# Engine per small SBUF step named in the list, and the list planned anew with a VectorE/GpSimd lock

## Chip, cores and metric

One core of one Trainium2 chip runs the kernel. The metric is the time of one execution on the device in microseconds (us), as the median of several runs. Engines are named as in the profile: PE is TensorE (PEld its weight loads), DVE is VectorE, ACT is ScalarE, POOL is GpSimd, SP is SyncE, which issues nearly all DMAs.

## The reference

Two blocks are chained. The first is a linear attention with decay, over 4 batches, 8 heads, 768 tokens and head size 48; its output is read as a 3072 x 384 matrix, which the second block feeds through a multiplicative feed-forward net (width 1024).

```python
for t in range(S):                                     # S = 768, all in float32
    cur = einsum('bhd,bhe->bhde', u * k[t], v[t])
    y[t] = einsum('bhd,bhde->bhe', r[t], state + cur)
    state = w * state + einsum('bhd,bhe->bhde', k[t], v[t])
x = y.transpose(0, 2, 1, 3).reshape(B * S, H * D)      # 3072 x 384
out = (((x @ w1) * (x @ w2)) @ w3) @ w_out             # 384 -> 1024 -> 1024 -> 384
```

## The kernel before

**Attention.** The 24 units are 6 chunks of 128 tokens by 4 batches, and unit n is visited once. Its k, r and v are loaded by SP (`kr.n`, `v.n`). Step `k.n` (`scale`, L459) multiplies k and r by powers of the decay, one 128x768 product of two SBUF operands. The results are turned so that the head dimension lies on the partitions: on PE for the first five units (`T`, `R`, with `t`, `r` on ACT), later by 32x32 blocks on DVE (`x`), a round trip through DRAM on SP (`y`, `z`) and a copy on ACT (`l`). PE then forms the sums for the state (`U`) and the pair products (`A`); DVE updates the state (`i`, `j`, each with a product of two SBUF operands at L633 in all but the first chunk's first half) and masks the pairs (`m`); PE multiplies by the state (`S`) and by the pairs (`V`), with a small fence on DVE in between (`fe`, L720). For units from 5 on the term of u is made apart: `d.n` and `e.n` (L468 and L471, 128x384 products, k r u), `f.n` (sums per head on DVE) and `g.n` (eight ACT scalings of v, or for unit 5 one DVE product, `h.5`). `vs.n` (L715) copies the odd heads' v to the other half of the partitions. `Y`, `yt` and `yx` add up, turn and store the unit's output as columns of x.

**Weights.** The inputs of the feed-forward net arrive as pairs of 32-bit words. Each of the 32 pieces (8 of 768 columns for w1 and w2, 8 of 384 for w_out, 16 of 512 for w3) is fetched by SP into one of three buffers (`W.i`, L272), and converted in five steps: `M` and `L` on ACT, `N` (L419), `H` (L422) and `Q` (L429, an addition of integers of two SBUF operands) on DVE. The w3 pieces are turned on DVE (`G`) and multiplied with w_out on PE (`F`, L445).

**Feed-forward net.** Chunk 0 uses plain products (`a`, `b`). Chunks 1 to 5 use a scheme with twenty products for eight blocks (`pa`, `pb`, L949), which needs 22 sums of weight blocks for each of w1 and w2 (`wa`, `wb`) and 11 sums of token blocks for each chunk (`xs`), all 128x256 sums of two SBUF operands (L921). `ga` and `gb` take the products out of PSUM, on ACT and DVE. The last product uses seven for eight (`P`, L834), with sums of 128x512 blocks of two SBUF operands (`s`, L816 and L819), and `E` takes it out. `D` stores.

**What sets the order.** Everything after the set-up follows one list written out by hand of a planner, `ORDER`: 1580 words such as `k.4` or `S.5/20` (after the slash, PSUM banks). Each engine issues its own instructions strictly in the order of the list, and waits by semaphores only. The engine of a step is fixed in the code of the step: `scale`, `total` (Q) and the masks run on DVE; `rk`, `rku` (d, e), `odd_values` (vs), `sum_of_ab` (s) and `sums_of_x` (xs) on POOL; `sums_of_w` alternates, even sums on DVE, odd ones on POOL; `place` (g) runs on ACT. `ps` (L934) sets up three PSUM banks just ahead of the first `pa`; it ends the early part of the list.

Of the kernel before, what the change touches and what calls it, by code (L numbers as in the profile page):

```python
# [29 lines left out]
N.3 L.4 a.0.1.0/1 H.3 Y.2/23 W.7 Y.3/05 k.4 yt.2/2 L.3 yt.3/3 b.0.0.0/0 yx.2/2 Q.3 W.6 c.0.1.0/1 yx.3/3 R.4/5 j.2/4  # L30
M.5 a.0.2.2/2 N.5 H.5 Q.4 L.5 a.0.1.1/1 Q.5 W.8 M.7 N.7 b.0.2.2/3 c.0.2.2/2 kr.7 H.7 u.0.0.0/0 L.7 N.6 M.6 T.4/4 Q.7
W.10 a.0.4.2/2 c.0.1.1/1 H.6 M.8 ub N.8 L.6 H.8 k.5 L.8 W.9 b.0.1.0/0 t.4/4 Q.6 a.0.5.2/1 W.11 x.5 M.10 e.5 N.10 H.10
v.5 L.10 y.5 r.4/5 b.0.5.2/4 Q.10 W.13 M.9 Q.8 c.0.5.2/1 N.9 ku.4 H.9 u.0.2.2/3 L.9 U.4/51 vs.5 M.11 A.4 W.12 k.6
c.0.4.2/2 Au.4 a.0.0.1/3 N.11 H.11 cz.1 L.11 Q.9 b.0.3.2/2 M.13 W.14 u.0.1.0/0 f.5 N.13 d.6 M.12 Q.11 kr.8 N.12 H.13
e.6 a.0.3.2/0 z.5 u.0.5.2/4 L.13 i.4/5 H.12 W.16 x.6 L.12 a.0.6.2/4 c.0.3.2/0 f.6 M.14 m.4 d.7 W.15 Q.13 wb.1 N.14
H.14 b.0.6.2/5 vs.4 j.4/1 L.14 l.5 Q.14 W.17 mo.4 M.16 Q.12 S.4/01 y.6 N.16 c.0.6.2/4 v.6 U.5 H.16 A.5 fe.4/1 M.15
N.15 V.4/01 L.16 H.15 b.0.4.2/4 u.0.3.2/2 L.15 W.19 Q.15 u.0.6.2/5 M.17 W.18 i.5 Y.4/01 c.0.0.1/3 a.0.7.2/2 N.17 m.5
j.5 z.6 k.7 yt.4/5 H.17 b.0.7.2/0 yx.4/5 u.0.4.2/4 L.17 Q.16 W.20 Q.17 G.0 b.0.1.1/1 M.18 v.7 N.18 c.0.7.2/2 F.0/3
N.19 H.18 x.7 L.18 M.19 W.21 h.5 H.19 Q.18 L.19 M.20 N.20 W.22 Q.19 vs.7 H.20 vs.6 b.0.0.1/5 G.1 y.7 L.20 e.7 l.6 W.23
u.0.7.2/0 F.1/4 M.21 N.21 u.0.0.1/5 H.21 Q.20 L.21 M.22 N.22 W.24 wa.0 H.22 Q.21 L.22 X.0/3 G.2 W.25 U.6 f.7 S.5/20  # L40
M.23 A.6 cz.0 d.8 N.23 F.2/5 H.23 k.8 L.23 g.6 W.26 i.6 Q.22 Q.23 z.7 M.24 G.3 M.25 N.25 kr.9 F.3/3 H.25 N.24 L.25
H.24 X.2/5 W.28 Q.25 M.26 X.1/4 fe.5/0 N.26 L.24 H.26 m.6 L.26 j.6 l.7 W.29 Q.24 S.6/54 X.3/3 x.8 U.7 W.27 A.7 fe.6/4
G.4 V.5/20 V.6/54 M.28 y.8 Q.26 F.4/3 kr.10 m.7 Y.5/20 N.28 M.29 u.0.1.1/1 H.28 N.29 L.28 H.29 W.31 Q.28 L.29 Q.29
wb.3 yt.5/2 X.4/3 P.0.1.0/0 e.8 G.6 yx.5/2 M.27 N.27 F.6/1 H.27 k.9 L.27 W.30 i.7 Q.27 G.5 v.8 z.8 wa.2 x.9 F.5/3
# [1075 lines left out]
```

## Time and profile before

| | |
|---|---|
| median of 3 runs (us) | 487.74 (484.59 to 488.23) |
| the profiled execution: its own time | 482.68 |
| its span, first to last instruction | 480.9 |
| busy: PE, DVE, ACT, POOL (us) | 454.3, 313.4, 200.6, 187.0 |
| mean granted clock of PE | 0.994 |

Busy time is that of an engine's own instructions. PE's matmuls are pipelined, so a busy PE need not run at its peak. The chain of waits is the list of work that ended last, followed back from the end. A window's "DMA share" is the busy share of the sixteen DMA engines. The rows the prediction uses stand in a section of their own below.

### The profile page before, as it was taken

What the parts mean: (1) busy time and instruction counts of PE and PEld (TensorE: products, weight loads), DVE (VectorE), ACT (ScalarE), POOL (GpSimd) and SP (SyncE); (2) the same over time, 40 slices, a digit from 0 to 9 for tenths busy, and PEclk for the clock granted to TensorE, in tenths of its full rate; (3) what the DMA queues carried; (4) which work ended last, traced back from release to release, by engine and by line L of the source; (5) the groups of instructions that cost most, each with busy time, mean ns of one, the idle gap of its engine ahead of it and who ended that gap; (6) DMA issues with size and microseconds to landing.
All of it is one profiled execution on the core that took longest, in us unless ns stands there. A gap on an engine that the chain in (4) does not pass through costs nothing.

```text
span 480.9 us, 12217 instructions
## 1 busy us (share of the span) xinstructions
PE 454.3 (94%) x4977; PEld 377.6 (79%) x4977; DVE 313.4 (65%) x596; ACT 200.6 (42%) x451; POOL 187.0 (39%) x228
## 2 busy tenths in 40 slices
...
GB/s 183 272 225 260 205 192 231 230 185 211 208 86 149 155 12 132 66 134 65 90 47 180 72 108 73 99 116 1 91 25 35 33 19 50 1 16 1 49 20 56
DMA packets 100482, 52.74 MB, mean 110 GB/s; under 512 B 79296, under 2 KB 89792, under 8 KB 100416
## 3 DMA queue, kind: packets, MB, share of 16 engines
...
q14 instruction: 25, 0.20, 0.1%
q10 hardware_dynamic: 624, 0.00, 0.1%
...
## 4 chain that ended last, share of the span: by engine, by line
PE 60%; DVE 18%; DMA 10%; issue 4%; ACT 3%; SPq 3%; POOL 0%; DVEq 0%; ACTq 0%
PE ps_fixed L949 22%; DMA raw<-in_moe_w_dram 7%; PE ps_b L949 6%; PE ps_a L949 5%; PE ps_s3t L834 3%; PE ps_s4b L834 3%; PE ps_a12b L834 3%; PE ps_a22t L834 3%; PE ps_s1t L834 2%; PE ps_a11b L834 2%; PE ps_s2t L834 2%; ACT t L426 2%; SPq L272 2%; DVE krs L459 2%; PE ps_y L708 2%
## 5 line engine op out<-in xcount | busy, mean ns | idle before, releaser
L816 POOL TENSOR_TENSOR raw<-abt,abt 128x512 f32<-128x512 f32 x12 | 16.5, 1379 | 144.6 <-DVE abt L982 129.9
L949 PE MATMUL ps_fixed<-xT,w 128*128 128x256 f32 x200 | 50.8, 381 | 0.0
L445 PE MATMUL ps_w<-wo,w3T 128*128 128x384 f32 x128 | 43.0, 490 | 2.1 <-DVE w3T L440 1.8
L949 PEld LDWEIGHTS ps_fixed<-xT,w 128*128 128x128 f32 x200 | 37.2, 190 | 4.8 <-ACT ps_fixed L966 0.5
L489 ACT ACTIVATE ynat<-vnat,dg 128x48 f32<-128x48 f32 x144 | 34.6, 330 | 14.9 <-PE ps_x L747 12.5
L445 PEld LDWEIGHTS ps_w<-wo,w3T 128*128 128x128 f32 x128 | 23.8, 190 | 18.6 <-ACT w3n L414 1.7
L715 POOL COPY vodd<-vnat 64x192 f32<-64x192 f32 x48 | 19.8, 412 | 45.4 <-DMA vnat<-in_v_dram 39.6
L468 POOL TENSOR_TENSOR ruk<-krin 128x384 f32<-128x384 f32 x19 | 21.5, 1129 | 37.7 <-DVE dg L475 26.7
L982 DVE TENSOR_TENSOR abt<-ps_fixed,abt 128x512 f32<-128x512 f32 x35 | 24.1, 688 | 16.2 <-PE ps_fixed L949 16.0
L426 ACT ACTIVATE t<-raw 128x512 uint32<-128x512 uint32 (+2 forms) x32 | 22.8, 714 | 24.1 <-DVE w3n L422 11.2
L980 ACT COPY abt<-ps_fixed 128x512 f32<-128x512 f32 x30 | 17.4, 589 | 29.9 <-PE ps_fixed L949 29.9
L459 DVE TENSOR_TENSOR krs<-krin,pn_in 128x768 f32<-128x768 f32 x24 | 26.4, 1104 | 1.6 <-ACT pn_in L342 1.1
L471 POOL TENSOR_TENSOR ruk<-ruk,ub 128x384 f32<-128x384 f32 x19 | 19.6, 1031 | 17.6 <-DMA ub<-in_u_dram 16.5
L545 ACT COPY kT<-tt 128x1024 f32<-128x1024 f32 x19 | 19.9, 1045 | 9.0 <-PE ps_y L708 4.2
L777 PE MATMUL ps_a<-xT,w 128*128 128x512 f32 (+1 forms) x60 | 22.6, 516 | 0.2
L777 PE MATMUL ps_b<-xT,w 128*128 128x512 f32 (+1 forms) x60 | 22.2, 509 | 0.0
L753 ACT COPY xT<-ps_x 128x384 f32<-128x384 f32 x24 | 11.4, 479 | 24.6 <-PE ps_x L747 14.6
L949 PE MATMUL ps_b<-x,w 128*128 128x256 f32 x80 | 20.8, 383 | 0.3 <-DVE ps_fixed L976 0.2
L949 PE MATMUL ps_fixed<-x,w 128*128 128x256 f32 x80 | 20.6, 380 | 0.0
L949 PE MATMUL ps_a<-x,w 128*128 128x256 f32 x80 | 20.6, 380 | 0.0
L834 PE MATMUL ps_a12b<-w,abt 128*128 128x192 f32 x96 | 18.7, 342 | 1.2 <-DVE u L862 1.2
L819 POOL TENSOR_TENSOR raw<-abt,raw 128x512 f32<-128x512 f32 x12 | 16.2, 1352 | 8.2 <-DVE abt L982 7.5
...
## 6 DMA issues: line engine op xcount, KB each, us to landing
...
```

The costliest lines, as they stand in the source:

```text
L426: nc.scalar.activation(out=part["t", i], in_=words(i)[0], func=COPY, scale=2.0 ** -29)
L445: nc.tensor.matmul(ps, lhsT=w3T[j][:, kc].rearrange("x b k -> x (b k)"), rhs=wo[kc], start=(kc == 0), stop=(kc == KF - 1))
L459: nc.vector.tensor_mul(krs[n % NS][:, which, :, :D], kr[:, which], pn[:, which, :, :D])
L468: (nc.gpsimd if fast else nc.vector).tensor_mul(ruk[n], krin[n % NIN][:, 0], krin[n % NIN][:, 1])
L471: (nc.gpsimd if fast else nc.vector).tensor_mul(ruk[n], ruk[n], ub)
L489: nc.scalar.activation(out=ynat[n][:, h, :], in_=vnat[n % NV][:, h, :], func=COPY, scale=dg[n][:, h:h + 1])
L545: nc.scalar.copy(out=turned(n).rearrange("x g p (z t) -> x (g p) z t", t=Q), in_=tts.rearrange("x z e t -> x e z t"))
L715: nc.gpsimd.tensor_copy(out=vodd[n % NV][rows(a)], in_=vnat[n % NV].rearrange("t (p i) d -> t i p d", i=2)[rows(1 - a), 1])
L777: nc.tensor.matmul(ps, lhsT=(w1 if x == "a" else w2)[:, z, q, js], rhs=xT[c][:, q, ts], start=(q == 0), stop=(q == KM - 1))
L834: nc.tensor.matmul(ps, lhsT=operand(c, j // 2, a)[:, j % 2, m * C:(m + 1) * C], rhs=w34[:, KH * (x == 1) + j, :DH] if x < 2 else made[b][: ...
L949: nc.tensor.matmul(bank_of(w, c, n)[:, i * TH:(i + 1) * TH], lhsT=of_weights(w, of_w)[:, i * P:(i + 1) * P], rhs=of_tokens(c, of_x), start ...
L982: nc.vector.tensor_mul(at(*more), flat(ps), at(*more))
```

## The change

Each word of the list can now carry an engine: `k.1@g` on GpSimd, `k.2@V` on VectorE, `vs.0@A` on ScalarE. The steps that read it are `k`, `Q`, `d`, `e`, `g`, `vs`, `s`, `wa`, `wb` and `xs`. The list has been planned anew by a planner that knows of a lock between VectorE and GpSimd; the whole order changes with it. The set of steps is the same but for `h.5`, which is now `g.5@V`, and two new steps: `Z.4` and `Z.3`, seven idle matmuls of `ident` by itself at the start (`busy_array`, in the code before, not used in the list). The numbers of steps by engine, before and after:

| step | DVE | POOL | ACT |
|---|---|---|---|
| k (24) | 24 to 12 | 0 to 12 | |
| Q (32) | 32 to 19 | 0 to 13 | |
| d, e (19 each) | 0 to 9, 0 to 10 | 19 to 10, 19 to 9 | |
| s (48) | 0 to 19 | 48 to 29 | |
| xs (55) | 0 to 18 | 55 to 37 | |
| wa, wb (44) | 22 to 25 | 22 to 19 | |
| g (19) | 1 to 7 | | 18 to 12 |
| vs (24) | | 24 to 14 | 0 to 10 |

```diff
 ORDER = """
-v.1 kr.2 W.1 uw k.1 k.0 T.1/0 T.0/1 N.0 M.0 R.0/2 W.2 U.0/34 r.0/2 H.0 vs.1 kr.3 t.0/1 R.1/5 i.0/3 vs.0 ku.0 U.1/21
-j.0/4 A.0 S.0/34 k.2 L.0 Au.0 i.1/2 r.1/5 W.3 m.0 t.1/0 S.1/25 mo.0 v.2 ku.1 R.2/0 N.1 A.1 j.1/1 M.1 Q.0 H.1 M.2 Au.1
...
+kr.2 k.1@g W.1 v.1 vs.0@A k.0 Z.4/1 T.0/0 R.0/1 t.0/0 R.1/2 N.0 M.0 T.1/3 uw U.0/45 v.2 r.0/1 H.0 A.0 W.2 L.0 k.2@V
+kr.3 ku.0 i.0/4 Z.3/1 T.2/0 Q.0@V S.0/14 j.0/5 Au.0 M.1 N.1 t.1/3 H.1 vs.1@A U.1/53 W.3 L.1 i.1/5 ku.1 W.4 Q.1@g j.1/3
...
+Q.20@g G.1 c.0.1.1/0 kr.8 N.22 F.1/2 wb.0@g u.0.5.2/1 M.21 H.22 vs.5@g wa.0@V L.22 N.21 l.6 x.7 W.25 Q.22@g M.23 f.7
+H.21 y.7 N.23 L.21 H.23 b.0.1.1/4 X.0/5 Q.21@g u.0.4.2/3 L.23 b.0.0.1/0 W.26 Q.23@g G.2 M.25 S.5/15 W.24 X.1/2 d.8@V
...
+        chosen_banks, chosen_side = [], [""]
+        sides = dict(V=nc.vector, A=nc.scalar, g=nc.gpsimd)
+        side = lambda other: sides.get(chosen_side[0], other)
...
         def total(i):
-            nc.vector.tensor_add(part[i], part[i], part["t", i])
+            side(nc.vector).tensor_add(part[i], part[i], part["t", i])
...
-                nc.vector.tensor_mul(krs[n % NS][:, which, :, :D], kr[:, which], pn[:, which, :, :D])
+                side(nc.vector).tensor_mul(krs[n % NS][:, which, :, :D], kr[:, which], pn[:, which, :, :D])
...
-            (nc.gpsimd if fast else nc.vector).tensor_mul(ruk[n], krin[n % NIN][:, 0], krin[n % NIN][:, 1])
+            side(nc.vector).tensor_mul(ruk[n], krin[n % NIN][:, 0], krin[n % NIN][:, 1])
...
-            if engine is nc.vector:
+            if side(nc.scalar) is nc.vector:
                 nc.vector.tensor_mul(ynat[n], vnat[n % NV], dg[n][:, :, None].to_broadcast([C, H, D]))
...
-                nc.gpsimd.tensor_copy(out=vodd[n % NV][rows(a)], in_=vnat[n % NV].rearrange("t (p i) d -> t i p d", i=2)[rows(1 - a), 1])
+                (nc.scalar.copy if side(nc.scalar) is nc.scalar else nc.gpsimd.tensor_copy)(out=vodd[n % NV][rows(a)], in_=vnat[n % NV].rearrange("t (p i) d -> t i p d", i=2)[rows(1 - a), 1])
...
-            engine = nc.gpsimd if fast else nc.vector
+            engine = side(nc.vector)
...
-            add_up((nc.vector, nc.gpsimd)[x % 2], WSUMS, x, lambda n: of_weights(w, n))
+            add_up(WSUMS, x, lambda n: of_weights(w, n))
...
-            add_up(nc.gpsimd, XSUMS, x, lambda n: of_tokens(c, n))
+            add_up(XSUMS, x, lambda n: of_tokens(c, n))
...
                     word, _, at = word.partition("/")
+                    word, _, chosen_side[0] = word.partition("@")
```

## Rows read from the trace of the kernel before

**Rows 1.** Windows: length, busy us (instructions) of PE, PEld, DVE, ACT, POOL; clock; DMA share, GB/s
```profile
12.00:74.60 62.60, 56.13 (x936) 36.76 (x935) 56.45 (x96) 41.63 (x86) 12.70 (x18) 1.00 0.87 232
74.60:126.00 51.40, 49.64 (x403) 30.35 (x402) 49.08 (x85) 25.74 (x51) 6.88 (x8) 1.00 0.86 209
126.00:169.00 43.00, 37.77 (x708) 31.84 (x706) 39.01 (x72) 19.53 (x57) 36.05 (x39) 0.96 0.60 145
169.00:474.00 305.00, 301.63 (x2887) 270.54 (x2886) 161.73 (x309) 110.24 (x255) 126.97 (x147) 1.00 0.22 61
```

**Rows 2.** Timeline: the last Q of w_out on DVE, the last of `ps` on PE
```profile
74.03 0.55 DVE L429 CUSTOM_DVE_ANT_0 wo<-wo,t 128x768 uint16<-128x768 uint16 x1
...
168.74 0.38 PE L934 MATMUL ps_fixed<-ident 128*128 128x512 bf16 x1 [1.01 <-DVE osb_low L858]
```

**Rows 3.** Waits of PE from 74.6 to 169 us: total, times, longest
```profile
PE ps_y L731 <- DVE AT L720: 2.0, 1, 2.0
PE ps_w L445 <- DVE w3T L440: 1.8, 3, 0.7
PE ps_fixed L934 <- DVE osb_low L858: 1.0, 1, 1.0
PE ps_s3t L834 <- DVE w L804: 0.8, 1, 0.8
```

**Rows 4.** Windows around the one fall of the clock
```profile
138.40:141.80 3.40, 2.15 (x66) 2.06 (x67) 3.34 (x6) 0.00 (x0) 1.63 (x2) 0.80 0.54 120
141.80:144.00 2.20, 2.20 (x9) 2.20 (x8) 2.17 (x5) 2.14 (x9) 2.20 (x3) 0.53 0.00 0
```

**Rows 5.** DVE by line: ns min/median/max, first and last start, forms
```profile
L459 DVE TENSOR_TENSOR krs<-krin,pn_in x24: 940/951/2042, 9.2 to 368.7; 128x768 f32<-128x768 f32 x24
...
L429 DVE CUSTOM_DVE_ANT_0 w3n<-w3n,t x16: 651/684/1529, 79.4 to 127.6; 128x1024 uint16<-128x1024 uint16 x16
...
L422 DVE SCALAR_TENSOR_TENSOR wo<-wo,t x8: 546/559/559, 47.3 to 72.8; 128x384 uint32<-128x384 uint32 x8
...
L633 DVE TENSOR_TENSOR half<-half,wn_in x20: 358/359/1446, 63.7 to 398.2; 128x192 f32<-128x192 f32 x20
...
L921 DVE TENSOR_TENSOR wa<-w x3: 412/483/943, 151.4 to 182.2; 128x256 f32<-128x256 f32 x3
```

**Rows 6.** The same view of POOL
```profile
L819 POOL TENSOR_TENSOR raw<-raw,abt x12: 1272/1275/1447, 136.7 to 457.8; 128x512 f32<-128x512 f32 x12
...
L468 POOL TENSOR_TENSOR ruk<-krin x19: 995/1001/1798, 33.1 to 334.7; 128x384 f32<-128x384 f32 x19
...
L468 POOLq MODIFY_POOL_CONFIG x2: 3/3/3, 26.8 to 26.9; - x2
...
L921 POOL TENSOR_TENSOR x<-x,xT x25: 721/730/902, 151.7 to 413.8; 128x256 f32<-128x256 f32 x25
```

**Rows 7.** Groups of DVE from 126 to 180 us: count, busy us, mean ns, idle
```profile
L921 DVE TENSOR_TENSOR raw<-w 128x256 f32<-128x256 f32 x3 | 3.4, 1145 | 0.1
L633 DVE TENSOR_TENSOR half<-half,wn_in 128x192 f32<-128x192 f32 x5 | 3.1, 615 | 0.2
L921 DVE TENSOR_TENSOR w<-w 128x256 f32<-128x256 f32 x3 | 2.9, 951 | 1.2 <-POOL w L921 1.2
L429 DVE CUSTOM_DVE_ANT_0 w3n<-w3n,t 128x1024 uint16<-128x1024 uint16 x2 | 2.2, 1107 | 0.1
L921 DVE TENSOR_TENSOR w<-w,raw 128x256 f32<-128x256 f32 x2 | 2.2, 1100 | 0.0
L633 DVE TENSOR_TENSOR st<-st,wn_in 128x192 f32<-128x192 f32 x4 | 2.0, 500 | 0.1
```

**Rows 8.** Window of the same stretch, columns as in the first group
```profile
126.00:180.00 54.00, 47.60 (x814) 40.22 (x813) 48.57 (x87) 22.85 (x63) 44.97 (x50) 0.97 0.48 116
```

**Rows 9.** Timeline of POOL: its first copies, its first product of two operands
```profile
12.07 2.22 POOL L715 COPY vodd<-vnat 64x192 f32<-64x192 f32 x4 [6.88 <-DMA vnat<-in_v_dram]
...
33.14 1.80 POOL L468 TENSOR_TENSOR ruk<-krin 128x384 f32<-128x384 f32 x1 [6.25 <-DMA krin<-in_r_dram]
```

212 lines of the change are left out of this document (107 added, 105 removed).

## The prediction

> **What bounds the kernel now.** I read the windows first [rows 1], cut where the list has two natural borders: 74.6 us, when the last integer sum of w_out ends, and about 169 us, when `ps` ends and the twenty products of chunk 1 begin [rows 2]. Call the stretches A (to 74.6), B (74.6 to 169) and C (169 to 474). The reader is to see that C and the rest are different kernels. In C, PE is busy 301.63 of 305.00 us and DVE only 161.73: PE sets the end, and all that a better order can win there is 3.4 us. In A and B the two are nearly equal: DVE 56.45 of 62.60, then 49.08 of 51.40 and 39.01 of 43.00, while PE idles 6.5, 1.8 and 5.2 us. POOL has 12.7, 6.9 and 36.1 us, so it stands nearly empty until 126 us, just where DVE is full. The DMA engines are the third party there, with shares of 0.87 and 0.86.
>
> Next, PE's waits in B [rows 3]: the four that end on DVE sum to 2.0 + 1.8 + 1.0 + 0.8 = 5.6 us, of the 7.0 us that PE idles there. The longest, 2.0 us on the fence of unit 7, is followed by the one fall of the granted clock, to the lower of its two levels (1.2 instead of 2.4 GHz): 0.80 over 3.40 us and 0.53 over 2.20 us [rows 4] are 0.20 x 3.40 / 0.5 + 0.47 x 2.20 / 0.5 = 3.4 us at half speed, or 1.7 us of lost work. So what DVE's lateness costs PE in B is about 7.3 us.
>
> Last, the durations. The 128x768 scaling takes 951 ns on DVE as a median but up to 2042; the 128x192 product of two SBUF operands 359 but up to 1446 [rows 5]. POOL's 128x512 sum takes 1275 ns, its 128x384 product 1001, its 128x256 sum 730 [rows 6], so POOL needs 1.8 times DVE's time. The long cases are DVE instructions with two SBUF operands that meet one of POOL's. From 126 to 180 us, six groups of DVE [rows 7] exceed their undisturbed durations [rows 5] by 3 x 0.73 + 5 x 0.26 + 3 x 0.54 + 2 x 0.42 + 2 x 0.69 + 4 x 0.14 = 7.9 us, against 44.97 us of POOL's work [rows 8]: each microsecond of POOL held DVE for 0.18 us or a little more.
>
> **The change part by part.** The set of steps stays, so PE's matmuls stay but for the seven idle ones of `Z`. These stand at the start, where PE waits for the first loads; if they were exposed they would cost seven 128x128 matmuls, under 2 us. I take nothing.
>
> *Prices.* For DVE I take 0.415, 0.559, 0.69 and 0.951 us for 256, 384, 512 and 768 columns [rows 5]. For POOL 0.730, 1.001 and 1.275 [rows 6], and 1.82 for 768 by going on at 0.274 us per 128 columns (an estimate). An integer sum on POOL isn't in the trace. Below, it is bounded by DVE's own 0.684 for 512 [rows 5], above by 1.80, the longest product of POOL shown [rows 6]; I take POOL's float price, the nearest row in engine and size.
>
> *Moves ahead of `ps`, counted over the two lists.* Off DVE go thirteen `Q` (eight of 512, two of 384, three of 768: 5.5 + 1.1 + 2.9 = 9.5 us) and six of thirteen `k` (5.7). On to it come ten `d` and `e` (5.6) and four `s` (2.8); one weight sum less is 0.4. That is -7.2 us. Steps that now stand behind `ps` (the last sum of folded weights, one unit's take, sums and fence) take 2.1 more off: -9.3, from 147.0 to 137.7 us. The PE steps in front of `ps` are the same but for two (`P.0.0.4` and `V.11`) that follow it now. POOL gets 17.7 us of `Q` and 10.9 of `k`, and loses eleven `d` and `e`, four `s`, fourteen copies of `vs` and one `xs`: +7.0, from 45.7 to 52.7.
>
> *By stretch.* In A, DVE's work hardly changes (59.8 to 59.1) while POOL's rises by 5.1 us, which at 0.18 costs DVE 0.9: A comes out at +0.2. In B, DVE goes from 87.2 to 78.7 and POOL from 35.9 to 37.8: 8.5 - 0.3 = 8.2 us of relief for DVE. PE can't use more than the 7.3 us that DVE's lateness costs it there. Against this, a new order has waits of its own: a result made on POOL is 0.3 to 0.9 us later than the same on DVE, and what follows it waits for that. For B I charge one new wait of the middle size of those listed, 1.0 us [rows 3]. B: -7.3 + 1.0 = -6.3.
>
> *In C* DVE gains 23.9 us of small steps (162.4 to 186.3 by prices) and POOL loses 32.8; with 305 us to lie in, both keep slack under PE's 301.63. If that cover were gone at a few points, the 3.4 us of idle would grow; if POOL's shorter list hands sums over sooner, it would shrink. I take zero, with -3.4 and +3.4 as bounds. The ten `vs` and the eight scalings fewer per moved `g` change ACT, which is busy 110.24 of 305 us in C and about half of B [rows 1]: hidden.
>
> *Sum.* +0.2 - 6.3 + 0 = -6.1 us on the profiled execution's 482.68 (span 480.9 and 1.8 around it): 476.6. The median of the runs shown is 487.74, 1.0% above that execution, so on the median's scale I predict 481.6.
>
> **One cost that the trace leaves open.** POOL's first product of two operands is preceded by two reconfigurations (MODIFY_POOL_CONFIG) at 26.8 to 26.9 us [rows 6], and starts only at 33.14, after 6.25 us of idle time that a load's landing ends [rows 9]. Whatever the reconfiguration itself took lay under that load. After the change POOL's first such instruction is `k.1@g`, and DVE started the scalings at 9.2 us [rows 5]. POOL is free from 12.07 - 6.88 = 5.2 us on [rows 9]. The cost is between nothing and all of the 6.25 us: then `k.1` ends at 5.2 + 6.25 + 1.82 = 13.3 us instead of 10.2, and PE's `R.1`, with everything behind it in its order, waits 3.1 us. I take nothing, since the trace names the load, and keep 3.1 as a rival. The Trainium skill (GPSIMD Engine Reference, Instruction dispatch) says that the first call of freshly loaded code pays about 6 us that no instruction of the profile shows; by it the full sum would be some 3 us higher (an estimate), and this trace can't tell, as the same gap holds a load.
>
> **The rivals.**
> *The early stretches give more.* With the lock known to the planner, A could also lose half of its idle 6.5 us and C half of its 3.4: -6.1 - 3.3 - 1.7 = -11.1, so 476.6. For it: POOL has room in A. Against: the DMA share of 0.87 in A, and a list whose DVE sum in A is the same.
> *DVE is relieved, something else ends the wait.* From 12 to 126 us the DMA engines are 0.86 to 0.87 busy, and PE is 49.64 of 51.40 in the first half of B: the relief of 8.2 us then shrinks to some 1 us, 486.7. Against: the waits listed end on DVE, not on loads.
> *The lock eats it (slower).* The net +7.0 us of POOL is the wrong measure if the work that it lost cost DVE nothing. New in the dense stretch are 17.7 + 10.9 = 28.6 us. If each microsecond of it holds DVE for a share h, DVE gains 9.3 - 28.6 h: it decides from h = 0.33. The rows average 0.18, but a single case reaches 2042 - 951 = 1.09 us behind a sum of 1.275. At h = 0.6 it is +7.9: 495.6. The Trainium skill (SBUF — State Buffer, Who interferes with whom) has the loser blocked for the whole instruction of the other engine, which leaves room for such an h.
> *The code load*: -6.1 + 3.1 = -3.0, 484.7.
> *The planned engines don't take effect* can't be: each word's engine is read where the step is issued.
>
> **How the numbers follow.** Chances: forecast 0.45, more 0.14, something else binds 0.19, the lock 0.14, the code load 0.08. About 1% is what a measurement here can tell from no change, and 1% below 487.7 is 482.9. The forecast's own range is 478 to 485, and most of it (0.36) lies below 482.9; with the second case's 0.14, faster has 0.50. Within 1%: 0.09 of the forecast, 0.17 of the third case and 0.07 of the code load: 0.33. Slower: the lock's 0.14, and 0.03 from the third and the last: 0.17. From 473 to 490 I leave out 0.1 at either end: below, the deepest part of the second case with C's bound; above, most of the lock's case.
>
> **What would show it.** Right: `ps` ends near 163 us instead of 169; DVE's busy share in B falls below 90%; no wait of PE on the fence over 1 us and no fall of the clock in B; C stays near 305 us with DVE near 185 busy; POOL's undisturbed `Q` of 512 near 1.28 us. Wrong: scalings and products of DVE whose mean in A exceeds 1.3 times the undisturbed one (the lock); POOL silent from 5 to about 11 us with PE waiting for `k.1` (the code load); PE's waits in B now on loads (something else binds); or `Q` on POOL far above 1.8 us, which would hold up w3's turning.

## The result and the profile after

The changed kernel takes 470.41 us as a median (469.6 to 471.82), the kernel before beside it 486.19: a ratio of 0.968 [0.962, 0.973]. Run again beside the last experiments it took 472.48 us (470.75 to 473.0) against 484.81: 0.975 [0.971, 0.980]; 469.5 to 472 us and 0.966 to 0.972 had been expected of that run. So the gain is 12 to 16 us, 2.5 to 3.2%. The prediction had the sign, but 481.6 us with a range from 473 to 490 is too slow: a gain of 6.1 us was forecast.

The windows of the changed kernel, columns as in [rows 1], the last border moved to where its `ps` ends:

```profile
12.00:74.60 62.60, 57.63 (x943) 38.77 (x944) 55.38 (x101) 43.97 (x91) 14.47 (x14) 0.97 0.90 242
74.60:126.00 51.40, 51.05 (x418) 32.97 (x417) 46.45 (x85) 29.01 (x61) 21.04 (x19) 1.00 0.86 209
126.00:159.40 33.40, 30.92 (x657) 25.53 (x657) 30.40 (x66) 17.11 (x50) 20.83 (x21) 1.00 0.60 149
159.40:461.00 301.60, 301.35 (x2927) 272.64 (x2926) 179.08 (x353) 102.88 (x215) 94.25 (x102) 1.00 0.24 64
```

Beside [rows 1], the second row says most: PE is now busy 51.05 of 51.40 us where it had 49.64, with POOL at 21.0 instead of 6.9 us. The third stretch is 9.6 us shorter (33.4 against 43.0). The last is 3.4 us shorter (301.6 against 305.0) although it has 40 matmuls more (`P.0.0.4` and `V.11` now stand there).

The end of `ps` in PE's timeline, beside [rows 2], and PE's waits from 74.6 to 159.4 us, beside [rows 3]:

```profile
155.95 0.59 PE L942 MATMUL ps_fixed<-ident 128*128 128x512 bf16 x2
159.03 0.38 PE L942 MATMUL ps_fixed<-ident 128*128 128x512 bf16 x1 [2.48 <-DVE osb_top L871]
```

```profile
PE ps_fixed L942 <- DVE osb_top L871: 2.5, 1, 2.5
PE ps_w L452 <- DVE w3T L447: 0.3, 1, 0.3
```

Of the four waits of before, three are gone and one (for the turned w3) has 0.3 instead of 1.8 us. One new wait has come, on the bank that `E.0.0.7` frees. The fall of the clock [rows 4] has moved to 22 us, behind a wait of 1.98 us that ends on ScalarE's L524 (`r.1`, for which `U.2` waits):

```profile
22.00:25.30 3.30, 3.30 (x100) 3.18 (x93) 2.38 (x3) 3.30 (x9) 1.39 (x1) 0.50 0.97 363
```

The durations that answer [rows 5, 6] (ns min/median/max): POOL's scalings and integer sums, DVE's scalings and POOL's sum of folded weights:

```profile
L466 POOL TENSOR_TENSOR krs<-krin,pn_in x12: 1819/1830/2587, 9.2 to 349.2; 128x768 f32<-128x768 f32 x12
...
L466 DVE TENSOR_TENSOR krs<-krin,pn_in x12: 947/956/1823, 9.2 to 296.8; 128x768 f32<-128x768 f32 x12
...
L436 POOL TENSOR_TENSOR w3n<-w3n,t x8: 1277/1280/1423, 77.8 to 107.4; 128x512 uint32<-128x512 uint32 x8
L436 POOL TENSOR_TENSOR w<-w,t x3: 1809/1815/1817, 19.0 to 39.0; 128x768 uint32<-128x768 uint32 x3
```

An integer sum costs POOL what the float product of that size does (1280 against 1275 ns), and the estimate of 1.82 us for 768 columns holds (1815 and 1830).

**A measure for the rest.** Windows cut at a time don't hold the same work in two kernels. So I priced each matmul of the trace at its undisturbed length (0.109, 0.1625, 0.2155, 0.3225 and 0.429 us for 128, 192, 256, 384 and 512 columns, 0.0125 for 48 or 64 columns on 64 rows, nothing for idle ones), added them up in PE's order, and call the *lag* the time at which a point of this sum is reached, less the sum. The three stretches end at 50, 130 and 417 us of priced work, near the borders A, B and C of the prediction. What the clock took is told apart: each of its falls lasts 3.41 us or twice that, at half level, so it costs 1.7 or 3.4 us. All in us:

| kernel | lag in A | in B | in C | clock | sum |
|---|---|---|---|---|---|
| before | 25.6 | 12.6 | 16.7 | 1.7 | 56.6 |
| changed | 23.1 | 7.4 | 11.3 | 1.7 | 43.5 |
| changed, second profile | 22.5 | 7.0 | 11.3 | 5.1 | 45.9 |
| new list, old engines | 28.2 | 14.8 | 14.3 | 3.4 | 60.7 |
| old list, new engines | 26.6 | 18.1 | 18.0 | 13.7 | 76.4 |
| old engines ahead of `ps` only | 28.1 | 14.9 | 11.8 | 3.4 | 58.2 |
| old engines behind `ps` only | 23.6 | 6.6 | 14.4 | 1.7 | 46.3 |
| Q and early k back | 23.6 | 13.9 | 11.3 | 6.8 | 55.6 |
| early d, e, s, vs, weights' sums back | 24.7 | 10.5 | 11.6 | 5.1 | 51.9 |
| late g back | 24.8 | 7.2 | 14.3 | 3.4 | 49.7 |

Kernels with the same words show how far one profile can be trusted: those alike ahead of `ps` (changed twice, old engines behind `ps`, late g back) differ by 2.3 us in A and 0.8 in B, and those alike behind it by at most 0.5 in C. In the second profile of the changed kernel the new wait of 2.50 us is followed by a fall of the clock that the first did not have:

```profile
160.10:163.40 3.30, 3.30 (x98) 2.79 (x97) 0.00 (x0) 0.13 (x1) 0.00 (x0) 0.50 0.28 56
```

### The profile page after: what moved, and what is told of

Read it like the earlier page. It is cut to its first block, busy times and chain, and to the rows that moved or that the text cites. A ratio compares the mean times of both kernels' runs of the same rounds, so it can differ in the third digit from the quotient of the medians.

```text
span 467.8 us, 12206 instructions
## 1 busy us (share of the span) xinstructions
PE 449.7 (96%) x4991; PEld 377.6 (81%) x4991; DVE 317.3 (68%) x636; ACT 197.5 (42%) x423; POOL 157.5 (34%) x174
## 4 chain that ended last, share of the span: by engine, by line
PE 80%; DVE 7%; DMA 5%; ACT 2%; SPq 2%; issue 2%; POOL 1%; DVEq 0%; ACTq 0%; POOLq 0%
PE ps_fixed L957 24%; PE ps_w L452 8%; PE ps_b L957 7%; PE ps_a L957 7%; PE ps_a11b L841 3%; PE ps_s2t L841 3%; PE ps_a12b L841 3%; PE ps_s1t L841 3%; DMA raw<-in_moe_w_dram 3%; PE ps_a22t L841 3%; PE ps_s4b L841 3%; PE ps_s3t L841 3%; PE ps_y L738 2%; PE ps_y L715 2%; PE ps_a L588 2%; PE ps_a L595 2%
## 5 line engine op out<-in xcount | busy, mean ns | idle before, releaser
L466 POOL TENSOR_TENSOR krs<-krin,pn_in 128x768 f32<-128x768 f32 x12 | 22.9, 1911 | 18.0 <-PE ps_a L588 8.7
L826 POOL TENSOR_TENSOR raw<-raw,abt 128x512 f32<-128x512 f32 x10 | 13.0, 1306 | 40.1 <-DVE raw L823 37.7
L496 ACT ACTIVATE ynat<-vnat,dg 128x48 f32<-128x48 f32 x96 | 22.9, 325 | 7.8 <-DVE dg L482 6.1
L722 POOL COPY vodd<-vnat 64x192 f32<-64x192 f32 x28 | 11.5, 409 | 35.0 <-DMA vnat<-in_v_dram 30.4
L823 POOL TENSOR_TENSOR raw<-abt,abt 128x512 f32<-128x512 f32 x6 | 7.7, 1290 | 44.3 <-PE ps_s1t L841 30.5
L957 PE MATMUL ps_fixed<-x,w 128*128 128x256 f32 x80 | 20.6, 383 | 0.2 <-DVE ps_fixed L986 0.2
L957 PE MATMUL ps_b<-x,w 128*128 128x256 f32 x80 | 20.6, 381 | 0.0
L957 PE MATMUL ps_a<-x,w 128*128 128x256 f32 x80 | 20.6, 381 | 0.0
L760 ACT COPY xT<-ps_x 128x384 f32<-128x384 f32 x24 | 11.3, 481 | 19.9 <-PE ps_x L754 19.9
L536 DVE STREAM_TRANSPOSE tr<-krs 128x768 f32<-128x768 f32 x19 | 18.4, 969 | 1.4 <-DMA scratch<-tr 1.3
L784 PEld LDWEIGHTS ps_a<-xT,w 128*128 128x128 f32 x60 | 11.2, 190 | 9.4 <-issue 7.9
L646 DVE COPY_PREDICATED AT<-later,ps_a 128x512 f32<-128x512 int32 x24 | 17.5, 731 | 1.9 <-PE ps_a L616 0.9
```

Source lines behind the costliest of these rows:

```text
L466: side(nc.vector).tensor_mul(krs[n % NS][:, which, :, :D], kr[:, which], pn[:, which, :, :D])
L496: nc.scalar.activation(out=ynat[n][:, h, :], in_=vnat[n % NV][:, h, :], func=COPY, scale=dg[n][:, h:h + 1])
L536: nc.vector.transpose(out=blocks[n].rearrange("x m e t -> x e m t"), in_=krs[n % NS][:, :, :, :D])
L646: nc.vector.copy_predicated(AT[n], later.bitcast(I32)[:, None, None, :].to_broadcast([C, 2, NP, T]), upper(n))
L784: nc.tensor.matmul(ps, lhsT=(w1 if x == "a" else w2)[:, z, q, js], rhs=xT[c][:, q, ts], start=(q == 0), stop=(q == KM - 1))
L957: nc.tensor.matmul(bank_of(w, c, n)[:, i * TH:(i + 1) * TH], lhsT=of_weights(w, of_w)[:, i * P:(i + 1) * P], rhs=of_tokens(c, of_x), start ...
```

## The experiments

The theory at the start was the prediction's: time goes with VectorE's work, above all ahead of `ps`. The rivals: the list's order alone gives it; and the list and its engines only work as a pair, so that a step on another engine costs, whichever way the work moves.

**Order and engines apart.** `x1_order_alone` keeps the new list and gives each step its old engine; `x2_engines_alone` keeps the old list and gives each step its new one.

```diff
-kr.2 k.1@g W.1 v.1 vs.0@A k.0 Z.4/1 T.0/0 R.0/1 t.0/0 R.1/2 N.0 M.0 T.1/3 uw U.0/45 v.2 r.0/1 H.0 A.0 W.2 L.0 k.2@V
+kr.2 k.1@V W.1 v.1 vs.0@g k.0@V Z.4/1 T.0/0 R.0/1 t.0/0 R.1/2 N.0 M.0 T.1/3 uw U.0/45 v.2 r.0/1 H.0 A.0 W.2 L.0 k.2@V
...
```

> The new list in its new order, with every step back on the engine that it had before (k and Q on DVE, d, e, vs, s and xs on POOL, weight sums in turn, g on ACT). Theory 'engines' (the gain of 13 to 16 us comes from where the small steps run, so DVE is relieved ahead of ps and hands over sooner behind it): nearly all of it is lost, 482 to 488 us. Theory 'order' (the gain comes from the new order of the work, and the engines matter little): 470 to 475 us. Theory 'fit' (the order is only good for the engines it was planned for): slower than the kernel before, over 488 us.

Measured: 486.72 us, 1.004 [1.001, 1.008].

```diff
-v.1 kr.2 W.1 uw k.1 k.0 T.1/0 T.0/1 N.0 M.0 R.0/2 W.2 U.0/34 r.0/2 H.0 vs.1 kr.3 t.0/1 R.1/5 i.0/3 vs.0 ku.0 U.1/21
+v.1 kr.2 W.1 uw k.1@g k.0 T.1/0 T.0/1 N.0 M.0 R.0/2 W.2 U.0/34 r.0/2 H.0 vs.1@A kr.3 t.0/1 R.1/5 i.0/3 vs.0@A ku.0
...
```

> The list of before in its old order, with each step on the engine that the new list names for it. Theory 'engines': most of the gain is there, 472 to 478 us. Theory 'order': nothing, 484 to 489 us. Theory 'fit': results come late for an order that was not planned for them, over 489 us.

Measured: 498.67 us, 1.030 [1.025, 1.034], of which the clock takes 13.7 us in its profile. The first result lies in the range of 'engines', the second only in that of 'fit'. Neither half is worth anything; the old list even loses 3% by the new engines. It is the pair that gains 12 to 16 us.

**Where in time.** `x10_early_back` has the old engines ahead of `ps`, `x9_late_back` behind it, both in the new list.

```diff
-kr.3 ku.0 i.0/4 Z.3/1 T.2/0 Q.0@V S.0/14 j.0/5 Au.0 M.1 N.1 t.1/3 H.1 vs.1@A U.1/53 W.3 L.1 i.1/5 ku.1 W.4 Q.1@g j.1/3
+kr.3 ku.0 i.0/4 Z.3/1 T.2/0 Q.0@V S.0/14 j.0/5 Au.0 M.1 N.1 t.1/3 H.1 vs.1@g U.1/53 W.3 L.1 i.1/5 ku.1 W.4 Q.1@V j.1/3
...
```

> The changed kernel, with the steps ahead of ps back on their old engines and the late stretch left alone. By the prediction's sum DVE then has 9 us more to do ahead of ps, and PE waits 6 to 8 us longer for it: 476 to 479 us. By theory 'order': 470 to 473 us. By theory 'fit': over 480 us.

Measured: 484.96 us, 1.001 [0.998, 1.003], in the range of 'fit': the whole gain is lost, in A and B alone.

```diff
-wb.5@V V.11/15 pa.1.3/3 wa.20@V xs.1.6@V pa.1.1/0 v.14 ga.1.3/3 E.0.0.7/4 Y.11/15 pa.1.4/3 ga.1.1/0 wa.12@V B.3@V
+wb.5@g V.11/15 pa.1.3/3 wa.20@V xs.1.6@g pa.1.1/0 v.14 ga.1.3/3 E.0.0.7/4 Y.11/15 pa.1.4/3 ga.1.1/0 wa.12@V B.3@V
...
```

> The changed kernel, with the steps behind ps (the late stretch, where PE is busy all the time) back on their old engines and the early stretch left alone. If the 3.4 to 5 us that the late stretch gained come from sums and scalings that DVE hands over sooner than POOL: 474 to 477 us. If they come from the new order alone: 470 to 472 us. The prediction's sum (nothing to win behind ps) expects no change, 470 to 472 us.

Measured: 473.72 us, 0.979 [0.974, 0.983], 1.2 and 3.3 us above the two medians of the changed kernel. Its lag is 3.1 us longer in C (14.4 against 11.3), and elsewhere within the spread.

**One family at a time, ahead of `ps`.** 13 Q back to VectorE; 12 k (6 of them behind `ps`) back to VectorE; 19 d and e back to GpSimd (10 ahead of `ps`):

```diff
-Q.2@g R.3/0 ku.2 mo.1 yt.0/1 i.2/5 A.2 kr.5 N.3 M.3 S.1/45 Au.2 M.4 j.2/2 fe.1/5 H.3 W.5 V.1/45 Y.1/45 N.4 v.4 r.3/0
+Q.2@V R.3/0 ku.2 mo.1 yt.0/1 i.2/5 A.2 kr.5 N.3 M.3 S.1/45 Au.2 M.4 j.2/2 fe.1/5 H.3 W.5 V.1/45 Y.1/45 N.4 v.4 r.3/0
...
```

> The changed kernel with its 13 Q steps that had gone to GpSimd (all ahead of `ps`) put back on VectorE; list and all other engines as changed. Theory 1, VectorE's queue is what is paid: +13 x 0.69 us = 9.0 us of VectorE work before `ps`, so 478 to 481 us, and the lag grows between 60 and 150 us. Theory 2, the list is fitted to its engines and each departure costs about alike, whichever way the work moves: 13 of the 37 early steps that differ, so about 13/37 of the 14.5 us that all of them cost together, 475 to 476 us. Rival, the lock: 13 x 1.28 = 16.7 us less GpSimd work, fewer VectorE instructions that are held up, and 468 to 471 us.

Measured: 475.14 us, 0.980 [0.975, 0.985], in the range of theory 2.

```diff
-yt.1/2 k.4@g H.4 yx.0/1 U.3/45 yx.1/2 ub S.2/01 a.0.1.0/2 vs.3@g m.2 L.4 mo.2 t.3/3 W.7 i.3/4 L.3 a.0.0.0/3 j.3/5 ku.3
+yt.1/2 k.4@V H.4 yx.0/1 U.3/45 yx.1/2 ub S.2/01 a.0.1.0/2 vs.3@g m.2 L.4 mo.2 t.3/3 W.7 i.3/4 L.3 a.0.0.0/3 j.3/5 ku.3
...
```

> The changed kernel with its 12 k steps that had gone to GpSimd (6 ahead of `ps`, 6 behind it) put back on VectorE. Theory 1, VectorE's queue: 6 x 0.96 = 5.7 us more VectorE work before `ps`, half of it in the first 40 us where the fences of the first blocks queue behind it, so 475 to 477 us; behind `ps` nothing. Theory 2, fitted list: 6 of 37 early departures, 473 us. Rival, the lock: 6 x 1.83 = 11 us less GpSimd work ahead of `ps`, 468 to 470 us.

Measured: 476.97 us, 0.985 [0.982, 0.989], in the range of theory 1.

```diff
-W.13 M.11 N.9 a.0.7.2/5 Q.8@V H.9 e.6@V L.9 N.11 W.12 H.11 b.0.2.2/3 g.5@V L.11 Q.9@V W.14 Q.11@V u.0.1.0/4 M.13 f.6
+W.13 M.11 N.9 a.0.7.2/5 Q.8@V H.9 e.6@g L.9 N.11 W.12 H.11 b.0.2.2/3 g.5@V L.11 Q.9@V W.14 Q.11@V u.0.1.0/4 M.13 f.6
...
```

> The changed kernel with its d and e steps (10 ahead of `ps`, 9 behind it) put back from VectorE to GpSimd. Theory 1, VectorE's queue: 10 x 0.55 = 5.5 us less VectorE work before `ps`, so 465 to 470 us unless what waits for them comes late. Theory 2, fitted list: d and e now take about 1.2 us each on an engine that also holds Q and k, so their readers wait: 10 of 37 early departures, about 474 us, or more. Rival, the lock: 10 more GpSimd steps, 12 us of them, each holding up VectorE in part, 474 to 478 us; then VectorE's means rise, and under theory 2 they don't.

Measured: 474.1 us, 0.977 [0.974, 0.981]. Of its lag, 49.3 us, the clock has 6.8 (falls at 20, 75 and 164 us); without it 42.5 stand against 40.8 and 41.8 of the changed kernel. So Q costs some 3 us (44.5 without the clock's part), k some 5.5 (46.9), d and e no more than the spread of two profiles. VectorE's means do rise with d and e back, which theory 2 excluded: its step `H` of the w3 pieces has 830 instead of 726 ns (lines below).

The integer and folded sums (s, xs, wa, wb), then vs and the late g:

```diff
-L.29 kr.10 Q.29@V wa.2@g G.6 M.27 k.9@g y.8 Y.6/42 m.7 N.27 H.27 P.0.0.0/1 wa.3@V L.27 wb.3@V vs.7@A Q.27@V W.30
+L.29 kr.10 Q.29@V wa.2@V G.6 M.27 k.9@g y.8 Y.6/42 m.7 N.27 H.27 P.0.0.0/1 wa.3@g L.27 wb.3@g vs.7@A Q.27@V W.30
...
```

> The changed kernel with the integer sums (s, xs, wa, wb) on the engines they had: 12 steps ahead of `ps` differ (5 leave GpSimd, 7 go to it), and 44 behind it (41 go to GpSimd, 3 leave it). If a departure costs where it makes TensorE wait and nothing elsewhere: ahead of `ps` little, 0 to 2 us, as the reader of a sum is a product of much later; behind `ps` up to the 3 us that the late engines were worth together. So 470.5 to 474 us. If a departure from the engine that the list was planned with costs by itself, wherever it stands: 12 of 37 early ones, 5 us, and most of the 3 us behind `ps`, 476 to 479 us.

Measured: 473.62 us, 0.977 [0.974, 0.981]. In C the lag is 11.3, as in the changed kernel: 44 late sums on other engines cost nothing there. The 1.7 us that B has more are twice the spread there.

**Does VectorE's work set the price?** Q and the early k back together, 14.7 us more work on VectorE; and all other early steps back, 8 us less:

```diff
-kr.2 k.1@g W.1 v.1 vs.0@A k.0 Z.4/1 T.0/0 R.0/1 t.0/0 R.1/2 N.0 M.0 T.1/3 uw U.0/45 v.2 r.0/1 H.0 A.0 W.2 L.0 k.2@V
+kr.2 k.1@V W.1 v.1 vs.0@A k.0@V Z.4/1 T.0/0 R.0/1 t.0/0 R.1/2 N.0 M.0 T.1/3 uw U.0/45 v.2 r.0/1 H.0 A.0 W.2 L.0 k.2@V
...
```

> The changed kernel with the 13 Q and the 6 early k steps back on VectorE together: 9.0 + 5.7 = 14.7 us more work there ahead of `ps`. If VectorE's work is what is paid, one for one: 485 us. If their losses add up as they were seen one at a time (6.2 + 6.6 us of lag): 482 to 484 us. If they are the same waits and clock falls met twice: 475 to 479 us.

Measured: 479.57 us, 0.989 [0.986, 0.992], between the ranges of the second and the third case.

```diff
-kr.2 k.1@g W.1 v.1 vs.0@A k.0 Z.4/1 T.0/0 R.0/1 t.0/0 R.1/2 N.0 M.0 T.1/3 uw U.0/45 v.2 r.0/1 H.0 A.0 W.2 L.0 k.2@V
+kr.2 k.1@g W.1 v.1 vs.0@g k.0 Z.4/1 T.0/0 R.0/1 t.0/0 R.1/2 N.0 M.0 T.1/3 uw U.0/45 v.2 r.0/1 H.0 A.0 W.2 L.0 k.2@V
...
```

> The changed kernel with the early steps other than Q and k back on the engines they had: d, e (10), vs (6), s (4) and sums of weights (8). VectorE has about 8 us less to do ahead of `ps` and GpSimd some 20 us more. If VectorE's work is what counts: 465 to 471 us. If these steps come too late from GpSimd for what waits for them: 475 to 477 us. If they cost only where GpSimd's work and Q and k meet on VectorE's port: 471 to 474 us here, and the 3 to 4 us stay an effect of the sum.

Measured: 477.97 us, 0.987 [0.983, 0.990], above all three ranges and nearest to the second. The windows from 12 to 169 us of these two and of the second profile of the changed kernel, in this order, columns as in [rows 1]:

```profile
12.00:169.00 157.00, 142.96 (x2013) 99.15 (x2011) 143.66 (x267) 90.06 (x198) 29.76 (x36) 0.97 0.74 197
```

```profile
12.00:169.00 157.00, 145.24 (x2108) 101.21 (x2109) 134.47 (x238) 87.06 (x190) 77.12 (x78) 0.97 0.78 197
```

```profile
12.00:169.00 157.00, 149.53 (x2136) 105.82 (x2137) 136.95 (x263) 92.95 (x205) 57.99 (x56) 0.97 0.77 199
```

With Q and k back VectorE is busier (143.66 against 136.95 us) and PE has 6.6 us less; its new waits are on VectorE's `w3T` (2.5 us) and `ynat` (1.6). With the others back PE has 4.3 us less; its new waits are on VectorE and on ScalarE (these are PE's waits of that kernel from 12 to 170 us):

```profile
PE ps_w L452 <- DVE w3T L447: 1.3, 2, 1.0
PE ps_y L715 <- ACT a L790: 1.3, 2, 1.2
```

VectorE's 134.47 us there look like relief, but PE is behind in this window, so it holds less of the work. These are the windows up to the point at which PE has done 130 us of priced work, in the kernel before, the changed one (first profile), the one with Q and k back and the one with the others back:

```profile
0.00:170.40 170.40, 153.91 (x2156) 108.35 (x2157) 151.37 (x287) 90.35 (x196) 61.34 (x84) 0.99 0.79 198
0.00:162.50 162.50, 151.41 (x2169) 107.78 (x2169) 139.32 (x286) 95.03 (x209) 63.30 (x72) 0.99 0.81 204
0.00:174.60 174.60, 157.21 (x2168) 111.78 (x2169) 152.89 (x307) 94.92 (x209) 34.12 (x53) 0.96 0.73 191
0.00:170.60 170.60, 155.79 (x2168) 110.55 (x2169) 141.40 (x274) 91.00 (x197) 84.18 (x96) 0.97 0.78 195
```

With the others back VectorE has 8 us of steps less and is still busy 2.1 us longer than in the changed kernel (141.40 against 139.32), because its steps take longer while POOL works. The same 16 `H` of w3 in the changed kernel, with d and e back and with all the others back:

```profile
L429 DVE SCALAR_TENSOR_TENSOR w3n<-w3n,t 128x512 uint32<-128x512 uint32 x16 | 11.6, 726 | 1.3 <-ACT w3n L421 0.8
L429 DVE SCALAR_TENSOR_TENSOR w3n<-w3n,t 128x512 uint32<-128x512 uint32 x16 | 13.3, 830 | 1.1 <-ACT w3n L421 0.3
L429 DVE SCALAR_TENSOR_TENSOR w3n<-w3n,t 128x512 uint32<-128x512 uint32 x16 | 14.9, 930 | 1.1 <-ACT w3n L421 0.3
```

To add such hold-ups up to that point, I take each VectorE instruction's time above the 10th percentile of its kind (same operation, tiles and shape) over all runs. Those that overlap one of POOL's exceed it by 14.0 us in the kernel before, by 5.8 to 8.9 in five profiles with the changed words ahead of `ps`, by 6.3 with Q and k back, by 11.6 with d and e back and by 15.4 with all the others back; those that overlap none, by 1.2 to 2.1 us in each. So of the 12 to 13 us that VectorE is busy less in the two profiles of the changed kernel, some 8 are shorter hold-ups, although POOL has slightly more to do (63.30 against 61.34 us).

Without the clock's part, the lag with Q and k back is 48.8 us and with the others back 46.8, that is 7.5 and 5.5 us above the mean of the two changed profiles (41.3); together 13.0, and all early engines back are 13.5 above it. So the losses add up. VectorE's steps aren't paid one for one: 14.7 us of them put back cost 7.5. The 8 us of steps taken off came back as hold-ups, so that run is no loss in spite of a relieved VectorE. How much of its 5.5 us is hold-ups, and how much is results that come late from POOL, was not taken apart; with d and e alone back the hold-ups grow too, VectorE stays as busy (139.38 us), and nothing is lost beyond the spread.

**Behind `ps`.** First vs and late g back, then the six late g alone:

```diff
-ga.2.7/1 f.17 vs.15@A pa.2.8/1 ga.2.6/0 E.1.0.3/5 l.14 P.1.0.4/5 ga.2.2/2 z.15 pa.2.10/1 E.1.0.4/5 P.1.0.5/5
+ga.2.7/1 f.17 vs.15@g pa.2.8/1 ga.2.6/0 E.1.0.3/5 l.14 P.1.0.4/5 ga.2.2/2 z.15 pa.2.10/1 E.1.0.4/5 P.1.0.5/5
...
```

> The changed kernel with vs (10 steps) back from ScalarE to GpSimd and six late g back from VectorE to ScalarE. If the 1.3 us wait for ScalarE's L974 behind `ps`, seen where all late engines are put back, comes from g: it is here too, with about 1.3 to 1.5 us in the late stretch, and none of the other one (1.2 us, for VectorE's L727); if it comes from the sums, d, e or k, the late stretch is as in the changed kernel. Ahead of `ps` six vs are 0.6 us each on an engine with room: 0 to 1 us. Time 470.5 to 473 us.

Measured: 476.09 us, 0.982 [0.978, 0.986], above the range, with 15.0 us of lag in C and both waits there.

```diff
-i.15 k.17@g x.16 yt.13/3 ga.2.13/2 pa.2.12/0 m.15 yx.13/3 y.16 pa.2.14/2 kr.18 g.14@V P.1.0.1/5 ga.2.16/1 ga.2.14/2
+i.15 k.17@g x.16 yt.13/3 ga.2.13/2 pa.2.12/0 m.15 yx.13/3 y.16 pa.2.14/2 kr.18 g.14@A P.1.0.1/5 ga.2.16/1 ga.2.14/2
...
```

> The changed kernel with six late g steps (g.14, 16, 17, 19, 20, 21) back from VectorE to ScalarE, and nothing else. If the late loss is g: both waits of TensorE are there again, 1.3 us for ScalarE's L974 and 1.2 us for VectorE's L727, and 473 to 474 us, about 3 us above the changed kernel beside it. If it was the late vs: no such waits, 470 to 472 us.

Measured: 475.81 us, 0.982 [0.976, 0.988], 3.3 us above the changed kernel beside it (474.25 to 476.61 against 470.75 to 473.0 us); 14.3 us of lag in C. PE's waits behind `ps` in this kernel:

```profile
PE ps_fixed L957 <- ACT ps_fixed L974: 1.3, 1, 1.3
PE ps_y L738 <- DVE AT L727: 1.2, 1, 1.2
```

ScalarE's timeline around the first of them, in this kernel and then in the changed one (second profile):

```profile
248.37 1.90 ACT L496 ACTIVATE ynat<-vnat,dg 128x48 f32<-128x48 f32 x8
250.17 0.46 ACT L760 COPY xT<-ps_x 128x384 f32<-128x384 f32 x1
250.53 0.58 ACT L974 COPY ps_fixed<-ps_fixed 128x512 f32<-128x512 f32 x1
```

```profile
247.61 0.47 ACT L760 COPY xT<-ps_x 128x384 f32<-128x384 f32 x1
248.29 0.57 ACT L974 COPY ps_fixed<-ps_fixed 128x512 f32<-128x512 f32 x1 [0.21 <-ACT xT L760]
```

One g on ScalarE is eight instructions and 1.90 us, and the copy for which PE waits (L974) stands behind it in ScalarE's queue. The second wait comes of another g by way of VectorE. There `f` (L482), which writes a buffer `dg` that g reads, waits for ScalarE's g, and the fence (L727) for which PE waits stands behind `f`:

```profile
296.49 0.55 DVE L482 TENSOR_REDUCE dg<-ruk 128x8 f32<-128x384 f32 x1 [3.16 <-ACT ynat L496]
297.07 0.17 DVE L727 TENSOR_SCALAR AT<-ps_y 32x1 uint32<-32x1 uint32 x1
```

On VectorE a g is one instruction of 0.56 us, in a place where VectorE has room (seven in the changed kernel, six of them late):

```profile
L493 DVE TENSOR_TENSOR ynat<-vnat,dg 128x384 f32<-128x384 f32 x7 | 4.0, 566 | 1.9 <-PE ps_x L754 1.9
```

The same six g on VectorE in the old list with the old engines:

```diff
-P.1.0.1/0 ga.2.4/23 i.14 f.17 yt.13/2 pa.2.5/2 x.16 d.16 pa.2.10/3 E.1.0.1/0 ga.2.5/02 y.16 e.16 j.14 g.14 P.1.1.4/0
+e.16@g j.14 g.14@V P.1.1.4/0 m.14 pa.2.6/0 E.1.1.4/0 z.16 P.1.0.6/0 ga.2.6/0 yx.13/2 ga.2.10/13 U.15 A.15 pa.2.11/1
...
```

> The old list with the old engines, except that the six late g steps (g.14, 16, 17, 19, 20, 21) run on VectorE: one instruction of 0.56 us for eight of ScalarE that take 1.90 us. If g's length on ScalarE delays the copies of products in the old list too: about 3 us less than the kernel before, 0.994, and its waits of 1.2 us each for VectorE behind `ps` get shorter. If g costs only where the new list has put it: the same time within 0.3%, or slightly more, since VectorE's steps u and osb, for which TensorE waits there, queue behind six more steps.

Measured: 486.97 us, 1.005 [1.001, 1.008]: nothing gained. PE's two longest waits behind `ps`, in the kernel before and then here:

```profile
PE ps_x L747 <- DVE u L854: 1.2, 1, 1.2
PE ps_a12b L834 <- DVE u L862: 1.2, 1, 1.2
```

```profile
PE ps_x L754 <- DVE u L861: 2.2, 1, 2.2
PE ps_a12b L841 <- DVE u L869: 1.2, 1, 1.2
```

The first wait, for VectorE's `u`, grew by 1.0 us, and the clock fell behind it at 288 us. The old list has its late waits on VectorE, and six more steps there lengthen one of them. What a g costs is a matter of whose queue it stands in and what is behind it there.

**Can the rest be had?** The wait of 2.5 us at the end of `ps` and that of 2.0 us at 20.6 us are left in the changed kernel. `E.0.0.7` right behind `ps`; the same with `t.1` and `r.1` ahead of `M.1`; idle matmuls into the early wait; and these with `E.0.0.7`:

```diff
-l.12 e.11@g pa.1.0/3 Y.10/20 v.13 kr.13 j.11 xs.1.8@g ps/204 fe.11/5 f.11 U.12 ga.1.0/03 xs.1.3@V xs.1.5@g A.12 g.11@A
+l.12 e.11@g pa.1.0/3 Y.10/20 v.13 kr.13 j.11 xs.1.8@g ps/204 E.0.0.7/4 fe.11/5 f.11 U.12 ga.1.0/03 xs.1.3@V xs.1.5@g
...
```

> The changed kernel with E.0.0.7 right behind `ps` and nothing else moved. With it the wait for the third bank of `ps` fell from 2.5 to 1.7 us in one kernel and to 0.9 us in another: 0.8 to 1.6 us less than the changed kernel beside it, 468.5 to 470 us. If another step takes it over: the same time within 0.3%.

Measured: 471.35 us, 0.973 [0.969, 0.978], beside 0.975 [0.971, 0.980]. The wait is 1.4 instead of 2.5 us, the medians differ by 1.1 us, and the intervals overlap.

```diff
-kr.3 ku.0 i.0/4 Z.3/1 T.2/0 Q.0@V S.0/14 j.0/5 Au.0 M.1 N.1 t.1/3 H.1 vs.1@A U.1/53 W.3 L.1 i.1/5 ku.1 W.4 Q.1@g j.1/3
+kr.3 ku.0 i.0/4 Z.3/1 T.2/0 Q.0@V S.0/14 j.0/5 Au.0 t.1/3 r.1/2 M.1 N.1 H.1 vs.1@A U.1/53 W.3 L.1 i.1/5 ku.1 W.4 Q.1@g
...
```

> The changed kernel with three words of its list moved: E.0.0.7, which frees the bank that the third fill of `ps` is waiting for, to right behind `ps` (TensorE waits 2.5 us for it now), and t.1 and r.1 ahead of M.1 (ScalarE now holds them behind M.1, which waits for a load; TensorE waits 1.98 us, and its clock is at half level from 21.9 to 25.4 us, which costs 1.7 us more). If the time is set by the chain of TensorE's waits and these are not taken over by another: 2.5 + 2.0 + 1.7 = 6.2 us less at most, 464 to 467 us. Rival, each freed wait is taken over by the next in the queue (fe.11 and W behind E.0.0.7; M.1 is late by t.1's and r.1's time, 0.7 us): 468.5 to 471 us.

Measured: 469.99 us, 0.969 [0.965, 0.973]. `U.2` does go on at 18.61 instead of 20.58 us, now ended by the fence (L634, 1.7 us), but PE then waits 1.5 us for another `kT` and 1.0 for `AT`, the clock falls at 21.5 us as it did, and the lag at the end of A is 25.4 us (24.8 to 26.6 in the kernels with the changed words there, the clock's part included).

```diff
-kr.3 ku.0 i.0/4 Z.3/1 T.2/0 Q.0@V S.0/14 j.0/5 Au.0 M.1 N.1 t.1/3 H.1 vs.1@A U.1/53 W.3 L.1 i.1/5 ku.1 W.4 Q.1@g j.1/3
+kr.3 ku.0 i.0/4 Z.3/1 T.2/0 Q.0@V S.0/14 j.0/5 Au.0 M.1 N.1 t.1/3 H.1 vs.1@A Z.16/5 U.1/53 W.3 L.1 i.1/5 ku.1 W.4
...
```

> The changed kernel with 16 idle matmuls (128x128, into a bank that is free) put ahead of U.1, where TensorE waits 1.98 us for ScalarE and its clock is at half level for 3.41 us from 21.94 us on. If the fall follows the wait, the clock stays full there and 1.7 us come back: 468 to 469.5 us. If it doesn't, the idle matmuls (0.11 us each at full clock, 1.8 us) hold up what comes behind them: 470 to 472 us.

Measured: 472.97 us, 0.976 [0.972, 0.981]. The clock stays at its upper level in the same window:

```profile
22.00:25.30 3.30, 2.32 (x109) 2.01 (x103) 2.66 (x6) 1.07 (x2) 0.00 (x0) 1.00 1.04 374
```

So the fall did follow the idle time. But the lag in A is 27.6 us, 1.0 above the highest of those with the changed words. PE's timeline shows why, first in the changed kernel and then here:

```profile
16.50 1.08 PE L588 MATMUL ps_u<-vnat,krs 64*64 64x48 f32 x32
```

```profile
16.39 3.84 PE L995 MATMUL ps_busy<-ident 128*128 128x128 f32 x32
20.29 0.68 PE L588 MATMUL ps_u<-vnat,krs 64*64 64x48 f32 x32
```

The idle matmuls (32 in the trace for the word's 16) took 3.84 us, twice what was reckoned, and stood one word too early: `U.1`, which had been ready at 16.50 us, ran at 20.29, and only `U.2` behind it was the one that waited. With the word in the right place this wasn't tried.

```diff
-kr.3 ku.0 i.0/4 Z.3/1 T.2/0 Q.0@V S.0/14 j.0/5 Au.0 M.1 N.1 t.1/3 H.1 vs.1@A U.1/53 W.3 L.1 i.1/5 ku.1 W.4 Q.1@g j.1/3
+kr.3 ku.0 i.0/4 Z.3/1 T.2/0 Q.0@V S.0/14 j.0/5 Au.0 M.1 N.1 t.1/3 H.1 vs.1@A Z.16/5 U.1/53 W.3 L.1 i.1/5 ku.1 W.4
...
-l.12 e.11@g pa.1.0/3 Y.10/20 v.13 kr.13 j.11 xs.1.8@g ps/204 fe.11/5 f.11 U.12 ga.1.0/03 xs.1.3@V xs.1.5@g A.12 g.11@A
+fe.10/0 V.10/20 l.12 e.11@g pa.1.0/3 Y.10/20 v.13 kr.13 j.11 xs.1.8@g ps/204 E.0.0.7/4 fe.11/5 f.11 U.12 ga.1.0/03
...
```

> The same with E.0.0.7 right behind `ps` as well. Its wait of 2.5 us was 1.7 us with the word there; what was gained, 0.8 us, adds to the kernel with the filled wait: 467 to 469 us. If the next word in VectorE's queue takes it over: as that kernel.

Measured: 471.81 us, 0.974 [0.970, 0.978]. None of the four can be told from the changed kernel, so there is no better version to show.

## Why the prediction failed, step by step

**A, forecast +0.2.** With the clock's part, the lag at the end of A was 25.6 us before and 24.8 and 25.9 after: -0.8 and +0.3. The number is right, and in part by luck. Without the clock's part A gained 2.5 and 3.1 us, hardly more than the spread of 2.3 there, and the falls of the clock in A, which the sum did not have, took 1.7 and 3.4 back. The 0.9 us charged because POOL would hold up VectorE more did not come: the hold-ups in A, added up as above, were 4.0 us before, and 0.9 to 1.7 in four of the five profiles with the changed words there, 4.1 in the fifth.

**B, forecast -6.3.** With the clock's part it was 14.3 us before and 7.4 and 8.8 after: -6.9 and -5.5. The size is right (`ps` ended at 159.4 and 160.6 us where "near 163" was named), and the waits went as the text had it: no wait on the fence, the w3 waits nearly gone, one new one. That was charged at 1.0 us and measured 2.5, and with it, in the second profile, a fall of the clock. The reason behind the number is only half right. The text made 8.2 us of relief for VectorE out of work moved to POOL, one for one, and charged 0.3 us for more hold-ups. Put back, that work costs about half its length (7.5 of 14.7 us), and the other early steps cost 5.5 us when they are put back, though VectorE then has fewer steps. The hold-ups in B did not grow but fell, from 9.9 us to 4.9 to 6.5 in those five. That each step pays where its reader doesn't wait, and where POOL and VectorE meet less, fits these runs; ahead of `ps` it is not shown step by step. The test "VectorE's busy share in B below 90%" missed as well: 46.45 of 51.40 and 30.40 of 33.40 us are 90 and 91%.

**C, forecast 0, bounds -3.4 and +3.4.** This step failed. C gained 5.4 us (16.7 to 11.3), the same in both profiles, and it is all that lies between the 6.1 us forecast and the 10.7 to 13.1 of the profiles, but for what falls of the clock take and give.
- The value: the moved `vs` and `g` "change ACT, which is busy 110.24 of 305 us in C and about half of B [rows 1]: hidden" is the sentence that was wrong. The busy share said nothing: in the new list a g of 1.90 us on ScalarE is on PE's path twice, once ahead of a copy and once ahead of `f` and the fence. In the old list it does look hidden, since the same six g on VectorE gain nothing there. Putting the six late g back on ScalarE gives back 3.0 of the 5.4 us; late sums, k, d and e give back nothing. The other 2.4 us come with the list (14.3 with the old engines, 16.7 before); which of its moves does it was not taken apart.
- The bound: 3.4 us was PE's idle time. A matmul behind a wait also takes 0.22 to 0.27 us longer in the profile than its price (worked out in C for the five waits of over 0.1 us of the kernel before), so these waits, 3.3 us, cost 4.5. A sum of idle time is too low a cap.

**The scale.** The forecast of 476.6 us was raised by 1.0%, from the profiled execution to the median of three runs, 487.74. Beside the later kernels the kernel before has medians of 484.15 to 485.11 us over 7 to 19 runs, 2.6 to 3.6 us lower. So this step put the forecast too high as well.

**The rivals.** "The early stretches give more" came nearest, with 476.6 on the scale of medians: it had some of C's idle time go, but for the lock's sake, and put more in A, where nothing came once the clock's falls are counted. "Something else ends the wait" fell: PE is busy 51.05 of 51.40 us with the DMA share still at 0.86. "The lock eats it" fell: VectorE's scalings have a median of 956 ns as against 951, the waits in B shrank, and the hold-ups became fewer. The lock is there: the longest scaling takes 1823 ns. The Trainium skill (SBUF — State Buffer, Who interferes with whom) says that a VectorE instruction with two SBUF inputs contends with a GpSimd one that reads SBUF; the trace agrees: this scaling, which has two, starts at 128.26 us, while a sum of POOL runs from 128.00 to 129.27, and is 0.87 us longer than the median. "The code load" fell. POOL's reconfiguration and its first scaling:

```profile
L466 POOLq MODIFY_POOL_CONFIG  x2: 11/11/11, 6.4 to 6.4; - x2
```

```profile
9.24 2.59 POOL L466 TENSOR_TENSOR krs<-krin,pn_in 128x768 f32<-128x768 f32 x1 [4.06 <-ACT pn_in L347]
```

`k.1` starts at 9.24 us, as VectorE's first scaling does (9.2), released by ScalarE; all that is left to see is that this one takes 2.59 instead of 1.83 us. The Trainium skill (GPSIMD Engine Reference, Instruction dispatch) puts the first call of freshly loaded code at about 6 us; here at most the 2.8 us from the reconfiguration to the start could hide it.
